# A 16 KiB SBUF-to-SBUF copy on the sync queue, behind the first x transfer

## The chip, the cores and the metric

The kernel runs on one core of a Trainium2 chip. The metric is device time in microseconds (us) of one execution. The kernel before takes 152.08 us, the median of three runs (152.06 to 152.09).

## The reference

```python
def setup_inputs():
    ...
    B, S, D = 512, 32, 640
    return {
        "x": _w((lambda *s: _rng.normal(s) * 0.05)(B, S, D)),
        "fx": _w((lambda *s: _rng.normal(s) * 0.05)(B, S, D)),
        "alpha": _w((lambda *s: _rng.normal(s) * 0.05)(1) * 0.1),
    }

def reference(x, fx, alpha):
    return x + alpha * fx
```

Everything is bf16. x and fx have 10,485,760 elements each, 20.97 MB; the output has the same size. alpha is one number. So 41.94 MB are read and 20.97 MB are written, with one multiply and one add for each element.

## The kernel before

The tensors are seen as 128 partitions with 81,920 elements each, which the code counts in units of K = 1024 elements: 80 units. x is cut into three tiles, `X`: units 0 to 32, 32 to 64 and 64 to 80. fx is cut into five, `FX`: 0 to 16, 16 to 32, 32 to 51, 51 to 67 and 67 to 80. Both kinds of tile have two buffers, so x 2 takes the buffer of x 0 and can be loaded only after x 0 has been stored; f 2 takes the buffer of f 0, f 3 that of f 1, f 4 that of f 2, each after the computation that used it.

The order of all the work is written out by hand in `PLAN`; nothing is rearranged:

```python
PLAN = """
x 0
a
f 0
f 1
x 1
c 0 0
f 2
c 1 0
s 0
f 3
x 2
c 2 1
f 4
c 3 1
c 3 2
s 1
c 4 2
s 2
"""
```

"x i" and "f j" load a tile, "c j i" computes where tile f j and tile x i overlap, "s i" stores, and "a" brings alpha to all partitions. A computation is one instruction on VectorE (DVE), line 92, which writes f times alpha plus x over the x tile. alpha (line 111) is loaded to one partition, multiplied by a row of ones on TensorE (line 115) and copied from PSUM to SBUF (line 117).

All transfers are issued by SyncE (SP), in the order of the plan, and share one DMA queue: lines 77 (x), 111 (alpha), 85 (f) and 104 (stores). Before an issue, SP waits for what the transfer needs, for example a buffer to come free, and everything behind it on SP waits as well. `X_CUTS` cuts the load of x 0 in two: four units (1 MiB in all, 8 KiB in each partition) and then the other 28. So the queue begins with x 0 (1 MiB), x 0 (7 MiB), alpha, f 0, f 1, x 1.

`done` collects the transfers and computations; at the end, an instruction on SP waits for all of them but the last store.

Of the kernel before, what the change touches and what calls it, by code (L numbers as in the profile page):

```python
# [2 lines left out]

# [4 lines left out]

ACT = mybir.ActivationFunctionType
ALU = mybir.AluOpType  # L10
F32 = mybir.dt.float32
BF16 = mybir.dt.bfloat16

K = 1024
P = 128


X = [(0, 32), (32, 64), (64, 80)]
FX = [(0, 16), (16, 32), (32, 51), (51, 67), (67, 80)]

X_CUTS = {0: (4,)}
PLAN = """
x 0
# [20 lines that stand above are left out]
@with_exitstack  # L44
def kernel(
    ctx: ExitStack,
    tc: tile.TileContext,
    x: bass.AP,
    fx: bass.AP,
    alpha: bass.AP,  # L50
    out: bass.AP,
):

    nc = tc.nc
    xv = x.flatten_outer_dims().rearrange("(p n) d -> p (n d)", p=P)
    fxv = fx.flatten_outer_dims().rearrange("(p n) d -> p (n d)", p=P)  # L60
    ov = out.flatten_outer_dims().rearrange("(p n) d -> p (n d)", p=P)
    assert xv.shape[1] == X[-1][1] * K == FX[-1][1] * K

    consts = ctx.enter_context(tc.tile_pool(name="consts", bufs=1))
    psum = ctx.enter_context(tc.tile_pool(name="psum", bufs=1, space=bass.MemoryType.PSUM))
    wide = ctx.enter_context(tc.tile_pool(name="wide", bufs=2))
    fs = ctx.enter_context(tc.tile_pool(name="fs", bufs=2))
    ctx.enter_context(tc.manual_schedule())

    xt, ft = {}, {}  # L70
    done = []

    def load_x(i):
        a, b = X[i]
        xt[i] = wide.tile([P, max(e - s for s, e in X) * K], x.dtype, tag="x", name="x_t")
        for c, d in pairwise((a, *X_CUTS.get(i, ()), b)):
            r = nc.sync.dma_start(  # L77
                out=xt[i][:, (c - a) * K : (d - a) * K], in_=xv[:, c * K : d * K]
            )
            done.append(r)  # L80

    def load_f(j):
        a, b = FX[j]
        ft[j] = fs.tile([P, max(e - s for s, e in FX) * K], fx.dtype, tag="f", name="f_t")
        r = nc.sync.dma_start(out=ft[j][:, : (b - a) * K], in_=fxv[:, a * K : b * K])
        done.append(r)

    def compute(j, i):
        (fa, fb), (xa, xb) = FX[j], X[i]
        a, b = max(fa, xa), min(fb, xb)  # L90
        piece = xt[i][:, (a - xa) * K : (b - xa) * K]
        r = nc.vector.scalar_tensor_tensor(  # L92
            out=piece,
            in0=ft[j][:, (a - fa) * K : (b - fa) * K],
            scalar=lanes["a_f"][:],
            in1=piece,
            op0=ALU.mult,
            op1=ALU.add,
        )
        done.append(r)  # L100

    def store(i):
        a, b = X[i]
        r = nc.sync.dma_start(out=ov[:, a * K : b * K], in_=xt[i][:, : (b - a) * K])
        done.append(r)

    lanes = {}

    def alpha_to_lanes():
        a_1 = consts.tile([1, 1], alpha.dtype, name="a_1")  # L110
        done.append(nc.sync.dma_start(out=a_1[:], in_=alpha[None, :]))  # L111
        ones = consts.tile([1, P], alpha.dtype, name="ones")
        nc.vector.memset(ones[:], 1.0)  # L113
        a_ps = psum.tile([P, 1], F32, name="a_ps")
        done.append(nc.tensor.matmul(a_ps[:], ones[:], a_1[:], start=True, stop=True))  # L115
        lanes["a_f"] = consts.tile([P, 1], F32, name="a_f")
        nc.vector.tensor_copy(out=lanes["a_f"][:], in_=a_ps[:])  # L117

    does = {"x": load_x, "f": load_f, "c": compute, "s": store, "a": alpha_to_lanes}
    for step in PLAN.split("\n"):  # L120
        if step:
            what, *of = step.split()
            does[what](*map(int, of))


    rest = nc.sync.nop(nofuse=True)
    info = mybir.DependencyInfo(mybir.DependencyClass.Sync, mybir.DependencyReason.DATA)
    for i in done[:-1]:
        tc.add_manual_dep(rest.ins, i.ins.name, info, reason="all but the last store")


# [1 line left out]
_INS = ['x', 'fx', 'alpha']  # L133
_OUTS = [((512, 32, 640), 'bfloat16')]


# [23 lines left out]
```

## Time and profile before

| what | value |
|---|---|
| time, median of three runs | 152.08 us |
| the profiled execution: span from its first instruction to its last | 150.2 us |
| the profiled execution: its own time | not recorded apart; the median is 1.9 us over the span |
| DVE busy | 86.8 us, 58% of the span |
| DMA queue, share of 16 engines' span | 98.1% |
| bytes moved | 62.92 MB, 419 GB/s over the span |
| DVE idle before its computations, until an f load landed | 25.5 us |
| SP's first and second issue (both parts of x 0) | 0.73 us for 0.38, 1.16 us for 0.42 |
| first part of x 0, from issue to landing | 4.8 us |

The profile shows one execution. Busy time is the time in which an engine's instructions ran; issuing a transfer is not counted as busy and stands as "SPq" in the chain and the timeline. A transfer's "landing" is when its semaphore says that all of it is there. "DMA share" in a stretch is the mean share of the core's 16 DMA engines that was covered by packets; a packet is put wholly to a short stretch, so the share can be over 1 there, and stretches of many packets are to be preferred. There is one core, and its granted TensorE clock is 1.000.

### The profile page before, as it was taken

The page shows a single profiled execution, that of the slowest core. Times are in us where ns is not written, and L with a number is a line of the kernel's source. Part 1 is how long each engine was busy: PE and PEld are TensorE (multiplying, and loading weights), DVE is VectorE, ACT ScalarE, POOL GpSimd, SP SyncE. Part 2 cuts the span into 40 slices and gives each one's busy share as a digit, 9 for nine tenths or more (in the row PEclk, how much of TensorE's full clock was granted, in tenths as well). Part 3 has the DMA queues.
Part 4 walks back from the last instruction along what each step waited for, and adds up shares of the span by engine and source line. Part 5 has one row for each costly group of instructions (what it writes and reads, how often), then busy time and mean ns, then how long its engine had stood idle before and what let it go on. Part 6 is the DMA issues. An engine that isn't in the chain of part 4 may idle for free.

```text
span 150.2 us, 78 instructions
## 1 busy us (share of the span) xinstructions
PE 0.2 (0%) x1; PEld 0.1 (0%) x1; DVE 86.8 (58%) x8; POOL 0.2 (0%) x4
## 2 busy tenths in 40 slices
PE   0000000000000000000000000000000000000000
PEld 0000000000000000000000000000000000000000
DVE  0000000049999999970399999106999999980000
POOL 0000000000000000000000000000000000000000
DMA  5997989999969696999696999999999969696994
GB/s 179 589 428 305 489 384 419 436 454 471 576 297 559 279 559 279 497 394 435 279 559 279 559 401 410 445 419 419 419 393 454 620 279 559 279 559 297 454 463 183
DMA packets 1730, 62.92 MB, mean 419 GB/s; under 512 B 194, under 2 KB 194, under 8 KB 194
## 3 DMA queue, kind: packets, MB, share of 16 engines
q1 hardware_dynamic: 1730, 62.92, 98.1%
HBM read 41.94 MB, written 20.97 MB: 419 GB/s over the span
## 4 chain that ended last, share of the span: by engine, by line
DMA 54%; DVE 35%; SPq 1%; issue 0%; DVEq 0%
DMA f_t<-in_fx_dram 54%; DVE x_t L92 35%; SPq L77 1%; SPq L111 0%; DVEq L92 0%
## 5 line engine op out<-in xcount | busy, mean ns | idle before, releaser
L92 DVE SCALAR_TENSOR_TENSOR x_t<-f_t,a_f,x_t 128x16384 bf16<-128x16384 bf16 (+3 forms) x6 | 86.5, 14438 | 25.5 <-DMA f_t<-in_fx_dram 25.5
L117 DVE COPY a_f<-a_ps 128x1 f32<-128x1 f32 x1 | 0.2, 159 | 21.5 <-PE a_ps L115 21.5
L113 DVE MEMSET ones<- 1x128 bf16 x1 | 0.2, 165 | 0.8 <-PEq L144 0.8
L115 PE MATMUL a_ps<-a,ones 1*128 1x1 bf16 x1 | 0.2, 158 | 22.2 <-DMA a<-in_alpha_dram 22.2
L144 POOL MEMSET const-bfloat16-1.0<- 128x1 bf16 x1 | 0.1, 103 | 0.0
L144 POOL MEMSET const-uint8-127<- 128x1 uint8 x1 | 0.1, 103 | 0.0
L115 PEld LDWEIGHTS <-ones 1*128 1x128 bf16 x1 | 0.1, 100 | 1.0 <-DVE ones L113 1.0
L144 POOL MEMSET const-float32-1.0<- 128x1 f32 x1 | 0.1, 100 | 0.0
L144 POOL MEMSET const-float32-0.0<- 128x1 f32 x1 | 0.1, 99 | 0.2 <-issue 0.2
## 6 DMA issues: line engine op xcount, KB each, us to landing
f_t<-in_fx_dram SPq DMA_DIRECT2D x3, 4096.0 KB, 35.6
x_t<-in_x_dram SPq DMA_DIRECT2D x1, 7168.0 KB, 21.3
f_t<-in_fx_dram SPq DMA_DIRECT2D x1, 4864.0 KB, 24.1
x_t<-in_x_dram SPq DMA_DIRECT2D x1, 4096.0 KB, 19.2
out_dram<-x_t SPq DMA_DIRECT2D x1, 4096.0 KB, 14.9
f_t<-in_fx_dram SPq DMA_DIRECT2D x1, 3328.0 KB
x_t<-in_x_dram SPq DMA_DIRECT2D x1, 1024.0 KB, 4.8
out_dram<-x_t SPq DMA_DIRECT2D x2, 24.7
```

Source lines behind the costliest of these rows:

```text
L77: r = nc.sync.dma_start(out=xt[i][:, (c - a) * K : (d - a) * K], in_=xv[:, c * K : d * K])
L92: r = nc.vector.scalar_tensor_tensor(out=piece, in0=ft[j][:, (a - fa) * K : (b - fa) * K], scalar=lanes["a_f"][:], in1=piece, op0=ALU.mult ...
L113: nc.vector.memset(ones[:], 1.0)
L115: done.append(nc.tensor.matmul(a_ps[:], ones[:], a_1[:], start=True, stop=True))
L117: nc.vector.tensor_copy(out=lanes["a_f"][:], in_=a_ps[:])
L144: nc = _bacc.Bacc("TRN2", target_bir_lowering=False, num_devices=1)
```

## The change

A tile `blank` of 16 partitions and 1024 bf16 elements is made. GpSimd (POOL) sets its first 512 elements in each partition to zero. Right after the first part of x 0 is issued, SP issues a copy of these 16 rows of 1 KiB onto the second half of the same tile. Nothing reads the second half. The copy waits for POOL's memset, and is one more transfer in `done`. On SP it stands second, ahead of the second part of x 0; the order of all else is kept. The changed kernel's lines are later by 4 to 6 from here on (77 becomes 81, the copy is 86, 85 becomes 91, 92 becomes 98, 104 becomes 110, 111 becomes 117).

```diff
@@ -18,6 +18,7 @@
 FX = [(0, 16), (16, 32), (32, 51), (51, 67), (67, 80)]
 
+HEAD = 16
 X_CUTS = {0: (4,)}
@@ -67,6 +68,9 @@
     ctx.enter_context(tc.manual_schedule())
 
+    blank = consts.tile([HEAD, 1024], x.dtype, name="blank")
+    nc.gpsimd.memset(blank[:, :512], 0.0)
+
     xt, ft = {}, {}
@@ -78,6 +82,8 @@
             )
             done.append(r)
+            if (i, c) == (0, 0):
+                done.append(nc.sync.dma_start(out=blank[:, 512:], in_=blank[:, :512]))
```

## The prediction

> **What bounds the kernel now.** I read the page first: engine totals, then the DMA totals, then the chain that ended last, then the DMA issues, and after that the stretches of the span.
>
> ```profile
> PE 0.2 (0%) x1; PEld 0.1 (0%) x1; DVE 86.8 (58%) x8; POOL 0.2 (0%) x4
> DMA packets 1730, 62.92 MB, mean 419 GB/s; under 512 B 194, under 2 KB 194, under 8 KB 194
> q1 hardware_dynamic: 1730, 62.92, 98.1%
> DMA 54%; DVE 35%; SPq 1%; issue 0%; DVEq 0%
> ```
>
> No compute engine is full; one DMA queue is, at 98.1% of 16 engines' span. What is missing, 1.9% of 150.2 us, is 2.9 us, and the ends of the span use that up: no packet moves before about 1.75 us or after about 149. So the engines hold a packet nearly all the time between. The chain names DVE for 35%, yet that is only who was followed back. Its steps show it:
>
> ```profile
> 1.99 30.16 DMA f_t<-in_fx_dram
> 32.28 17.30 DVE x_t L92
> 49.59 24.12 DMA f_t<-in_fx_dram
> 73.80 20.50 DVE x_t L92
> 94.31 26.12 DMA f_t<-in_fx_dram
> 120.46 14.08 DVE x_t L92
> ```
>
> The columns are start and duration. A DVE result frees a buffer, and a load is issued then, but it lands 24 to 26 us later, because it stands behind others in the queue: 4.9 MB alone needs 11.5 us at 434 GB/s. The queue is never dry at these hand-overs. At the end, the last store is issued at 134.6 (DVE ends at 134.54), while the store of 8.39 MB ahead of it can begin only when the f load ends near 119.5 and lasts 19.3 us, to 138.8: 4 us of cover.
>
> ```profile
> 6.00:68.00 62.00, 0.16 (x1) 0.00 (x0) 34.64 (x3) 0.00 (x0) 1.00 1.00 434
> 95.00:118.00 23.00, 0.00 (x0) 0.00 (x0) 15.16 (x2) 0.00 (x0) 1.00 1.01 435
> ```
>
> The last columns, DMA share and GB/s, show the full rate, 434, or 27.1 GB/s per engine. The 62.92 MB take 145.0 us at it; with 1.75 before, 3.5 us of the 150.2 are left for losses and for the last completion. The landings in the chain place them: the bytes queued up to the first f load (12.58 MB) should end at 30.7 and land at 32.15, lag 1.4; up to the third f load (30.15 MB) 71.2 against 73.71, lag 2.5; up to the fifth (50.33 MB) 117.7 against 120.44, lag 2.7. So about 1.4 us is start-up plus one completion, and 1.1 us is lost between 32 and 74.
>
> **The change part by part.**
>
> *The memset on POOL (16x512).* Its four neighbours of 128x1 took 0.10 us each, and a 1x128 one on DVE took 0.17. No row has 512 elements; below, 0.10; above, 4 x 0.17 = 0.66, all of it as if it scaled. I take 0.4, nearer the upper end since the row is longer. Nobody but the copy uses it. Its first user is an SP instruction, so it counts through the next step.
>
> *The wait on SP.* SP issues everything:
>
> ```profile
> 0.73 0.86 SPq L77 DMA_DIRECT2D x_t<-in_x_dram  x2
> 1.63 0.32 SPq L111 DMA_DIRECT2D a<-in_alpha_dram  x1
> 1.99 0.87 SPq L85 DMA_DIRECT2D f_t<-in_fx_dram  x2
> 2.90 0.45 SPq L77 DMA_DIRECT2D x_t<-in_x_dram  x1
> ```
>
> The copy is second and waits for POOL; behind it stand the rest of x 0, alpha, two f loads and x 1. DVE's first instruction starts at 0.81; if POOL starts its memset then too, it ends by 0.9 to 1.5. SP would be free at 1.16, so it waits 0 to 0.35 us, then takes 0.32 to 0.45 (any row here) to issue the copy. All five are 0.3 to 0.8 us later. The rest of x 0 would go out at about 1.8 instead of 1.16, and it needs about 1.0 us to reach the engines (first issue 0.73, first packet near 1.75), so it is there by 2.8 to 3.0. The engines hold the first x transfer, 1.05 MB, for at least 2.4 us, to 4.2. That hides the delay with 1.2 us to spare; with the cover gone, the cost would be what the memset takes beyond that. Alpha is behind x 0 in the queue anyway: its matmul starts at 22.24, and its result is wanted at 32.28. The f and x 1 loads have the 7.3 MB of x 0 in front of them. The issue at 49.59 and all later ones wait for DVE or a landing, and are not moved.
>
> *The copy on the queue.* This is the only part on the path. It moves 16 KiB: at 434 GB/s that is 0.04 us, if its rows are spread over 16 engines. Then the boundary between two transfers: four transfers end between 6 and 68 at 434 GB/s, and none of their ends shows as a gap; 434 against 435 over 62 us is 0.14 us, or 0.04 us each. Below: 0 (a loss of nothing if it falls into the start-up loss). Above: the unhidden first latency, 1.0 us. I take 0.04 + 0.04 = 0.08, from the boundary rows, since those are in the same queue under the same load and the first latency belongs to an empty queue.
>
> A rule of the Trainium skill speaks against that. The page "DMA: Bandwidth & Descriptors", section "Anatomy of one DMA — SWDGE (gpsimd) path", gives each DMA a fixed cost of about 2.0 us, and its "Rules for kernel authors" tell you to coalesce anything under 64 KB. Paid in series this would make 154.1 us. The trace does not agree for queued transfers: thirteen of them at 2.0 us would be 26 us, and 3.5 are there. The rule's cost can be in the latency of each without being in the throughput. The page "SBUF — State Buffer", section on the DMA port swizzle, gives partitions 0 to 15 only 104 GB/s, an estimate of 0.16 us for the 16 KiB; no run here shows that, and it would make 152.24.
>
> *The lists behind.* The final wait on SP covers one more transfer, which has landed some 140 us before; the load of f 3 also waits on its semaphore, some 60 us after it landed. Both 0. The copy's tile takes 2 KiB per partition ahead of the x and f tiles; the DVE rows (17.28 us for 16384 elements) stay as they are, and 4 us of cover at the end would hide a small change.
>
> *Sum.* Against the profiled execution, 150.2 + 0.08 = 150.3 us of span. The median of the three runs, 152.08, is 1.9 us over that span; the same 1.9 added gives 152.16. A measurement of this kernel can tell about 0.2%, 0.30 us, from no change, so this is no change.
>
> **The rivals.**
>
> *A. Few engines carry the rows (slower).* 1730 packets less 194 small ones are 1536, 12 x 128: a packet per row, for twelve transfers. The 194 are 12 x 16 and 2, so a 128-row transfer marks 16 completions and the one-row alpha transfer leaves two packets: one row goes to one engine. Where 16 rows go, no row tells: 1 per engine, 8 as in the large transfers, or 16 on one. Each row is 1 KiB / 27.1 = 0.038 us; sixteen on one engine make 0.60 us, and every later transfer waits for that engine: 152.08 + 0.64 = 152.7. It decides (0.30 us) from eight rows on one engine, if that is the one which ends last. Against it: the large transfers are spread evenly.
>
> *B. The copy drains the queue (slower).* A read from SBUF in place of one from HBM could stop each engine once for something like the first latency, 1.0 us: 153.1. For it: no SBUF to SBUF transfer is in the trace, and the loss of 1.1 us ends near the first change from loads to a store (about 73). Against it: the change back to loads near 92 costs next to nothing, since the lag only goes from 2.5 to 2.7.
>
> *C. A better start (faster).* The first transfer runs slowly:
>
> ```profile
> 1.70:2.70 1.00, 0.00 (x0) 0.00 (x0) 0.00 (x0) 0.00 (x0) 1.00 1.10 270
> 2.70:3.70 1.00, 0.00 (x0) 0.00 (x0) 0.00 (x0) 0.00 (x0) 1.00 0.90 369
> ```
>
> At 434 these two stretches would have moved 0.23 MB more, 0.5 us. If that is because the issues of the next five transfers fall into it, moving them by 0.3 to 0.8 us returns some: 152.08 - 0.5 + 0.08 = 151.7. Against it: a first read is slow anyway.
>
> *D. The loss between 32 and 74 goes (faster).* It is 1.1 us in a queue that has work. If it hangs on how many entries came before, two more per engine may move or remove it: 152.08 - 1.1 + 0.08 = 151.1. Nothing shown ties it to that.
>
> **How the numbers follow.** Forecast 0.50; A 0.20; B 0.08; C 0.13; D 0.09. Same 0.50, slower 0.28, faster 0.22. The forecast's own range is 152.0 to 152.3, from nothing paid, with a little drift, to four rows on one engine (0.15 + 0.04). The range over the cases goes from 151.4 (all of C) to 152.8 (all of A); outside are B and D, 0.17.
>
> **What would show it.** The copy's issue on SP near 1.2 to 1.6 us, with a POOL wait under 0.4; the next x issue near 1.8; DMA share near 1 from 4 to 6 us; the first f landing at 32.2 to 32.3 and each later landing moved by the same 0.1; 16 more packets of 1 KiB and 16 more small ones. A landing moved by 0.6 speaks for A, by 1 for B, an earlier one for C; a lag that stays near 1.4 after 74 speaks for D. I am wrong if a memset of over 1.9 us holds SP, or if the copy makes an engine wait for something that queued transfers do not.

## The result, and the profile after

| | before | after |
|---|---|---|
| time, median | 152.07 us (152.04 to 152.09, 4 runs) | 152.77 us (152.68 to 152.89, 4 runs) |
| ratio | | 1.0047, 95% interval 1.0035 to 1.0059 |
| span of the profiled execution | 150.19 us | 150.89 us |
| time of the profiled execution | not recorded apart | 152.68 us |

The changed kernel is 0.70 us slower, 0.47%. That lies in the predicted range (151.4 to 152.8), but near its upper end, and it is not the likeliest case, which was no change; a slower kernel had been given 0.28. The profiled span grew by the same 0.70 us.

From the page of the changed kernel: the engine totals, the packet counts, the queue.

```profile
PE 0.2 (0%) x1; PEld 0.1 (0%) x1; DVE 86.8 (58%) x8; POOL 0.7 (0%) x5
DMA packets 1762, 62.93 MB, mean 417 GB/s; under 512 B 210, under 2 KB 226, under 8 KB 226
q1 hardware_dynamic: 1762, 62.93, 97.4%
```

There are 32 more packets: 16 of 1 KiB (226 less 210) and 16 more small ones (210 against 194). The trace does not name a packet's engine, but each of the sixteen 1 KiB packets starts 5 to 7 ns after the start of a different one of the 16 completion marks of the first part of x 0 (rows from 4.55 to 5.28 us, each as another engine comes free). So the copy is one row and one completion mark on each of 16 engines. The engines are busy for 97.4% of the span instead of 98.1%: 3.9 us missing instead of 2.9.

The start of the changed kernel in its timeline (start, duration, engine, line):

```profile
0.74 0.51 POOL L72 MEMSET blank<- 16x512 bf16 x1 [0.29 <-POOLq L150]
0.74 0.38 SPq L81 DMA_DIRECT2D x_t<-in_x_dram  x1
1.28 0.57 SPq L86 DMA_DIRECT2D blank<-blank  x1
1.89 0.57 SPq L81 DMA_DIRECT2D x_t<-in_x_dram  x1
```

POOL's memset takes 0.51 us and ends at 1.25; SP, free at 1.12, waits 0.16 and issues the copy in 0.57. The second part of x 0 goes out at 1.89 instead of 1.16, 0.73 us later.

The chain of the changed kernel (start, duration):

```profile
2.89 30.39 DMA f_t<-in_fx_dram
33.40 17.30 DVE x_t L98
50.72 23.75 DMA f_t<-in_fx_dram
74.56 20.50 DVE x_t L98
95.08 26.00 DMA f_t<-in_fx_dram
121.10 14.09 DVE x_t L98
```

Landings are start plus duration. The first f load lands at 33.28 against 32.15 before, 1.13 later; the third at 74.47 against 73.71, 0.76 later; the fifth at 121.07 against 120.44, 0.63 later. So more than the whole loss is made before 33 us, and part of it comes back by 74.

The stretch from 4.5 to 9 us, where the engines go from the first part of x 0 to the second, first of the kernel before, then of the changed one; the last column is GB/s:

```profile
4.50:9.00 4.50, 0.00 (x0) 0.00 (x0) 0.00 (x0) 0.00 (x0) 1.00 1.16 501
```

```profile
4.50:9.00 4.50, 0.00 (x0) 0.00 (x0) 0.00 (x0) 0.00 (x0) 1.00 1.15 437
```

64 GB/s less over 4.5 us are 0.29 MB, or 0.66 us at 434 GB/s. Packets are put wholly to the stretch in which they start, so this is rough, but the place is plain.

The packets themselves say who is late. The trace has their starts and durations, and each engine writes one completion mark per transfer, so 16 marks give the times at which 16 engines finished it. Worked out from them, in us (the spread is the last less the first):

```
end of transfer      before: mean  last  spread   after: mean   last  spread
x 0, second part            21.73  22.09  0.56          22.67  23.22   0.95
f 2 (the third f load)      73.21  73.40  0.41          73.20  74.12   1.41
last store                 148.78 148.99  0.44         148.76 149.68   1.41
```

On the mean, the engines end as early as before. The slowest one ends 0.69 us later, and a landing follows the slowest engine: 33.28 us after a last mark at 32.91, 74.47 after 74.13. The start cost 0.94 us on the mean and 1.13 on the slowest; around the first store (60 to 76 us) the packets took 0.35 us more than at full rate on the mean, where they took 1.32 before, so about 1 us came back, but unevenly.

### The profile page after: what moved, and what is told of

Its sections match the earlier page's. It is cut to its first block, busy times and chain, and to the rows that moved or that the text cites. A ratio compares the mean times of both kernels' runs of the same rounds, so it can differ in the third digit from the quotient of the medians.

```text
span 150.9 us, 82 instructions
## 1 busy us (share of the span) xinstructions
PE 0.2 (0%) x1; PEld 0.1 (0%) x1; DVE 86.8 (58%) x8; POOL 0.7 (0%) x5
## 3 DMA queue, kind: packets, MB, share of 16 engines
q1 hardware_dynamic: 1762, 62.93, 97.4%
## 4 chain that ended last, share of the span: by engine, by line
DMA 53%; DVE 34%; SPq 1%; POOLq 0%; issue 0%; DVEq 0%
DMA f_t<-in_fx_dram 53%; DVE x_t L98 34%; SPq L81 0%; SPq L86 0%; POOLq L161 0%; SPq L117 0%; DVEq L98 0%; POOLq L150 0%
## 5 line engine op out<-in xcount | busy, mean ns | idle before, releaser
L72 POOL MEMSET blank<- 16x512 bf16 x1 | 0.5, 514 | 0.3 <-POOLq L150 0.3
```

The lines of the kernel that those rows point to most:

```text
L72: nc.gpsimd.memset(blank[:, :512], 0.0)
```

## The experiments

Twelve kernels ran. The question was which part of the change makes the loss between 4.5 and 9 us: the later issue of the second part of x 0, the SBUF source, or any small transfer between two large ones. In the diffs, `...` stands for unchanged lines. Every ratio is to runs of the kernel before taken together with that experiment.

**A delay without a copy.**

```diff
+            if (i, c) == (0, 0):
+                nc.gpsimd.memset(xt[0][:16, 4 * K : 4 * K + 1200], 0.0)
```

> There is no copy here. The second part of x 0 waits for a POOL memset of 1200 elements that it overwrites, so that it is issued near 1.9 us, as in the changed kernel (1.89), instead of 1.16. Theory T1 (the copy costs because the second part of x 0 is issued late): 152.6 to 152.9 us, first f landing near 33.2. Theory T2 (the SBUF source of the copy costs) and theory T3 (any small transfer at this place costs): no copy, so 152.0 to 152.2, first f landing near 32.2.

Measured: 153.32 us (153.07 to 153.74), ratio 1.0085 (1.0056 to 1.0113). Its chain:

```profile
0.73 1.11 POOLq L157
1.85 0.33 SPq L77
2.61 30.20 DMA f_t<-in_fx_dram
50.24 24.53 DMA f_t<-in_fx_dram
```

The second part is issued at 1.85 and the first f load lands at 32.81. With no copy in the queue, time is lost, and in all it is more than with one. T2 and T3 cannot explain that; T1 stands. Neither of its numbers was met, though: the time is above 152.6 to 152.9, and the first landing is 0.66 us later than before, not the 1.1 of the changed kernel. The third landing, at 74.77, is 1.06 later, so the rest was lost near the first store. A longer delay below puts the first landing at 33.16, 1.01 later, also without a copy. So the late issue is enough for a loss of this size; whether the copy adds some tenths at the start is not shown, since each kernel has one profile.

**A copy from HBM, with no wait.** The source is `xv[:HEAD, :512]` and there is no memset:

```diff
-    nc.gpsimd.memset(blank[:, :512], 0.0)
...
-                done.append(nc.sync.dma_start(out=blank[:, 512:], in_=blank[:, :512]))
+                done.append(nc.sync.dma_start(out=blank[:, 512:], in_=xv[:HEAD, :512]))
```

> The copy of 16 rows of 1 KiB stands at the same place, but reads x from HBM and waits for nothing, so the second part of x 0 is issued near 1.65. T1: half the delay, so 152.1 to 152.5. T2: 152.0 to 152.2, since nothing reads SBUF. T3: 152.6 to 152.9.

Measured: 152.23 us, ratio 1.0026 (0.9998 to 1.0053). The median lies in T1's range, but the ten runs went from 152.01 to 153.77, far apart for this kernel, and the profile is of one of 153.48. Three of them are 0.75 to 1.64 us above the 152.13 of the kernel before, the other seven within its range (151.81 to 152.64). The second part is issued at 1.63, which looks like an edge: some executions pay and most do not.

**The source cleared by DVE.**

```diff
-    nc.gpsimd.memset(blank[:, :512], 0.0)
+    nc.vector.memset(blank[:, :512], 0.0)
```

> As the changed kernel, but DVE clears the source, which should end near 1.1 us, so the copy waits little and the second part of x 0 is issued near 1.65. T1: between 152.1 and 152.5, like the copy from HBM. T2 and T3: 152.6 to 152.9, as the changed kernel.

Measured: 152.76 us (152.58 to 152.91), ratio 1.0039 (1.0029 to 1.0050). DVE ended at 1.11 and SP issued the copy at 1.17, but the issue took 0.57 us (that of the copy from HBM took 0.42), so the second part went out at 1.79 and not at 1.65. The time lies outside T1's range for this run and in that of T2 and T3. Alone this could not tell them apart, since the delay came out nearly as long as the changed kernel's; with the next run it can.

**The copy behind the second part.**

```diff
-            if (i, c) == (0, 0):
+            if (i, d) == (0, 32):
```

> The same copy, behind the second part of x 0 instead of the first. The queue is full when the engines reach it near 21.7 us. T1: 152.0 to 152.3 with 0.1 us for the copy itself. T2 and T3, if each engine loses something at any such transfer: 152.6 or more, with the loss between 21 and 24 us.

Measured: 152.04 us (151.71 to 152.20), ratio 0.9990 (0.9977 to 1.0002). The same copy in the same queue costs nothing that can be measured where it makes no large transfer late that is needed soon. (It was issued at 1.64, after the memset had ended, so SP did not wait for POOL here.) From its chain, the first f load lands at 32.26:

```profile
2.77 29.49 DMA f_t<-in_fx_dram
49.70 24.01 DMA f_t<-in_fx_dram
94.31 26.04 DMA f_t<-in_fx_dram
```

**The loss near 70 us: another issue apart.** This is in both kernels and was the ground of rival D.

```diff
+    after = mybir.DependencyInfo(mybir.DependencyClass.Sync, mybir.DependencyReason.DATA)
...
+    loads = {}
...
+        if j == 3:
+            tc.add_manual_dep(r.ins, loads[2].ins.name, after, reason="apart from s 0")
+        loads[j] = r
```

> The kernel before, with the load of f 3 held on SP until f 2 has landed (near 73.7 us instead of 67.2), so that it is no longer issued right behind the store s 0. Theory D1 (the loss of about 1.2 us per engine near 70 us comes from two issues back to back into a running queue): the loss shrinks, 150.7 to 151.4 us. Theory D2 (it belongs to the first store, whatever follows it): no change, 151.9 to 152.3.

Measured: 151.94 us, ratio 1.0001 (0.9991 to 1.0010). D1 falls. The load of f 3 was issued at 73.67, yet the packets of 60 to 76 us still took 0.90 us more than at full rate. What makes this loss stays open; that it belongs to the first store was not shown either.

**The later issues held back.** Alpha, and with it f 0, f 1 and x 1, waits for the landing of the first part; done once on the changed kernel and once on the kernel before.

```diff
+    after = mybir.DependencyInfo(mybir.DependencyClass.Sync, mybir.DependencyReason.DATA)
...
-        done.append(nc.sync.dma_start(out=a_1[:], in_=alpha[None, :]))
+        r = nc.sync.dma_start(out=a_1[:], in_=alpha[None, :])
+        tc.add_manual_dep(r.ins, done[0].ins.name, after, reason="first x has landed")
+        done.append(r)
```

> The changed kernel, with alpha, f 0, f 1 and x 1 held on SP until the first part of x 0 has landed (near 5.6 us). The second part of x 0 is still issued near 1.89. Theory T1a (the second part of x 0 itself is issued too late): 152.6 to 152.9, as the changed kernel. Theory T1b (the issues of alpha, f 0, f 1 and x 1 now fall together with the engines' step from the first part to the second and hold it up): 152.0 to 152.3, and the spread of the engines stays near 0.5 us.

> The kernel before with the same hold of alpha, f 0, f 1 and x 1, and no copy. T1a: 152.0 to 152.2, no change. T1b: no change or up to 0.5 us less, if the slow first rows of the first part come from those issues too.

Measured: 152.75 us, ratio 1.0053 (1.0036 to 1.0070), on the changed kernel; 152.04, ratio 1.0002 (0.9993 to 1.0011), on the one before. The loss stays with the burst of issues behind the second part held back: T1b falls, T1a stands.

**Other delays, without a copy.** The memset of the first experiment with 710, 2400 and 4790 elements. S1 and S2 are the two theories of the longer first part, the last experiment below.

> No copy; the second part of x 0 waits for a memset of 710 elements and is issued near 1.42 us (1.16 before; 1.63 took 152.0 to 153.8, 1.85 took 153.1 to 153.7). S1: with a price that grows with the delay, 152.1 to 152.5. S2: issued before the first packet at 1.74, so 151.9 to 152.2, as before.

> No copy; the second part of x 0 waits for a memset of 2400 elements and is issued near 2.9 us instead of 1.16 (1.85 with 1200 elements, which took 153.3 us). T1a: another 1.0 us of delay costs up to another 1.0 us: 153.9 to 154.6. T1b: the loss moves with the burst and does not grow: 152.5 to 153.4.

> No copy; the second part of x 0 waits for a memset of 4790 elements and is issued near 4.85 us, after the first engines have finished the first part (near 4.6). This asks why a delay to 2.85 cost no more than one to 1.85. Theory L3 (a transfer needs about 3 us from issue to full rate on all engines, always): the engines stand until about 7.9, so 155.0 to 155.4. Theory L1 (it needs about 1.0 us, as the first transfer does, and being late costs a further fixed step of 0.7 to 1.0): the engines stand until about 5.9, so 153.8 to 154.4.

Measured: issued at 1.44, 152.17 us, ratio 1.0005 (0.9994 to 1.0015); at 2.85, 153.01 (152.66 to 153.99), ratio 1.0075 (1.0049 to 1.0100); at 4.84, 154.28 (154.17 to 154.54), ratio 1.0150 (1.0133 to 1.0167). The first lies in both ranges and does not tell S1 from S2; it does show that a memset on POOL of 0.68 us (the changed kernel's took 0.51) costs nothing by itself. The second contradicts T1a as I had put it: one more microsecond of delay cost no more. It lies in T1b's range, but T1b had fallen with the held issues above. Its first f load, from its chain:

```profile
3.61 29.55 DMA f_t<-in_fx_dram
```

The third is in the range of L1, not of L3. Its chain:

```profile
0.73 4.10 POOLq L157
4.84 0.33 SPq L77
5.61 28.74 DMA f_t<-in_fx_dram
51.78 24.37 DMA f_t<-in_fx_dram
```

Set side by side, with the time at which the first engine begins a row of the second part and the longest of the 16 engines' first rows, from the packets (57,344 B take 2.12 us at full rate):

```
kernel           issued  first row  lead   longest first row   time
before             1.16       4.63  3.47                2.28   152.07
e11_delay_s        1.44       4.57  3.13                2.33   152.17
e2_hbm             1.63       4.63  3.00                2.74   152.23 (profile: 153.48)
e3_dve             1.79       4.69  2.90                3.12   152.76
e1_delay           1.85       4.58  2.73                3.24   153.32
after              1.89       4.64  2.75                3.28   152.77
e6_after_hold      1.89       4.77  2.88                3.10   152.75
e8_delay2          2.85       4.79  1.94                2.79   153.01
e12_dry            4.84       5.81  0.97                3.57   154.28
```

The lead is the time from the issue to the first row, in the one profiled execution of each kernel. With a lead of 3.1 us or more, each engine goes from one part to the other at full rate. With 2.9 or less, the first rows take up to 1.2 us longer, on some engines after a gap, and the time does not grow as the lead gets shorter: 153.32 at 2.73, 153.01 at 1.94. Only when the issue comes after the engines have finished (4.84) is the time in which they stand added to that: the first row begins 0.97 us after the issue, as in the very first transfer, about 1 us after the engines could have begun it.

**A longer first part.** `X_CUTS = {0: (8,)}` in place of `(4,)`, with the copy and without:

```diff
-X_CUTS = {0: (4,)}
+X_CUTS = {0: (8,)}
```

> The changed kernel with the first part of x 0 twice as long (8 units, 2 MiB, until about 7.1 us instead of 4.6), so that the second part, issued near 1.89, has 2.4 us more of cover. Theory S1 (the engines reach the end of the first part before the late second part is ready): 151.9 to 152.2, the loss is gone. Theory S2 (what counts is that the second part was issued after the engines had begun to move the first, at 1.74 us, however long the first part lasts): 152.5 to 153.4.

> The kernel before with the first part twice as long and no copy, as the control for the run above. Both theories: 151.8 to 152.2, since the second part is issued at 1.16.

Measured: with the copy 151.84 us (151.66 to 152.09), ratio 0.9977 (0.9967 to 0.9987); without 151.94, ratio 0.9995 (0.9985 to 1.0005). The chain with the copy:

```profile
1.27 0.57 SPq L86
1.89 0.62 SPq L81
2.94 29.50 DMA f_t<-in_fx_dram
49.87 23.88 DMA f_t<-in_fx_dram
94.36 26.04 DMA f_t<-in_fx_dram
```

The second part, of 6 MiB here, is issued at 1.89, exactly as in the changed kernel, but the engines come to it at 7.2 us, with a lead of 5.3. The first f load lands at 32.44 instead of 33.28. S1 stands, S2 falls: the loss needs both the late issue and the short cover. This kernel is also the fastest that ran, 0.23% under the kernel before. Why it is, when its control is not clearly faster, is not settled: in the two profiles the packets of 60 to 76 us lose 0.74 us with the copy and 1.19 without, and that loss moved by some tenths between most of these kernels.

## Why the prediction was right or wrong

**What bounds the kernel** was read rightly: the queue. A delay on it of 1.13 us at 33 us shows in the later landings, as 0.76 and 0.63, and DVE's hand-overs never became the limit.

**The memset and the wait.** Sized well: 0.51 us for 0.4, a wait of 0.16 us within 0 to 0.35, the second part issued at 1.89 for 1.8. The issue of the copy took 0.57 us, more than any row from which I took 0.32 to 0.45.

**The step that failed** is "That hides the delay with 1.2 us to spare". I took the time from an issue to the engines from the first transfer, 1.0 us, and called a transfer ready once that had passed. That first latency is real (0.97 us in the run with 4790 elements), but it is the time until the first packet, not the lead needed to go on at full rate. The runs put that lead at about 3 us for this load: free at 3.13, on the edge at 3.00, paid at 2.90. The changed kernel has 2.75. So the cover was short by a few tenths where I counted 1.2 us over, and a term that I had put at nothing cost 1.13 us at the first f landing and 0.70 in the time. Why a shorter lead costs anything stays open. I had named the wrong kind of proof too: "a memset of over 1.9 us" would have been needed by my sum, and 0.51 was enough.

**The copy on the queue.** 0.08 us was near: its rows took 46 to 48 ns, with a mark of 9 ns, and behind the second part it cost nothing measurable. The rule of the Trainium skill that spoke against the change ("DMA: Bandwidth & Descriptors", section "Anatomy of one DMA — SWDGE (gpsimd) path", a fixed cost of about 2.0 us per DMA, fitted there to transfers on GpSimd's path, while these are issued by SyncE) is not what was paid: the same DMA one place later was free.

**Rival A** gave 152.7, and 152.77 was measured, but the agreement is of the number alone. The rows went one to an engine. The Trainium skill says so as well: "DMA: Bandwidth & Descriptors", the section on why a DMA increments its semaphore by 16, has a transfer from the sync queue spread over the largest number of engines up to 16 that divides its rows. The sixteen 1 KiB packets and sixteen extra marks agree. The range of 151.4 to 152.8 held the result by luck: its upper end is the whole price of rival A, and what was paid is another cost that happens to be as large.

**Rival B** (the copy drains the queue) falls by the run with the copy behind the second part, and by the loss that appears with no copy at all. Its size, one first latency, was of the right order, but a late issue alone brings such a loss, with no read from SBUF.

**Rival C** falls: the first transfer is as slow when nothing at all is issued behind it before 4.84 us, in the run with 4790 elements (the last column is GB/s; 270 and 369 before):

```profile
1.70:2.70 1.00, 0.00 (x0) 0.00 (x0) 0.00 (x0) 1.00 (x1) 1.00 0.96 254
2.70:3.70 1.00, 0.00 (x0) 0.00 (x0) 0.00 (x0) 1.00 (x1) 1.00 0.96 393
```

**Rival D**: the loss near 70 us did shrink, by about 1 us on the mean, and by 0.4 us on the landing (the delay goes from 1.13 to 0.76). That is why a loss of 1.13 us shows as 0.70 in the time. What ties the two is not known. It would also account for the 1200-element delay being slower than the changed kernel: in its profile the packets of 60 to 76 us lose 1.10 us, not 0.35. That was read, not tested.

## What to carry to other kernels

A DMA queue that is never empty can still lose time where a transfer reaches it late: count the lead from the issue to the moment at which the engines come to it, and compare it with a lead that is seen to be free in a trace (here 3.1 us, for one load of 7.3 MB behind one of 1 MB), not with the latency of the first packet. A small transfer costs little in the queue; it costs by its place on the issuing engine, with the wait in front of it and its own issue time (0.57 us), when a large transfer stands behind it and the one ahead is short. When bytes bound a kernel, look at the slowest of the 16 engines: here the mean engine ended at the same time in both kernels.

## What the runs showed that was not expected

- Up to 2.85 us, the price looks like a step and not a slope: with the issue at 1.79, 1.85, 1.89 and 2.85 us the times were 152.76, 153.32, 152.77 and 153.01, and the first rows of the second part took up to 3.28 us instead of 2.12. Why a row is slow when its transfer was issued 1.9 to 2.9 us ahead, long after the 1.0 us in which a first packet can start, was not found.
- Engines that fall apart stay apart, but for the stretch around the first store. In the changed kernel a spread of 0.95 us made at the start was still 0.94 at 61 us, and the one of 1.41 at 74 us was 1.41 at the end.
- The issue of the copy from SBUF to SBUF kept SP for 0.57 us, and that of the load behind it for 0.57 as well, where the same load took 0.42 in the kernel before and 0.33 after a wait of its own.
